# Weights that begin 64 bytes behind a multiple of 2048 bytes in SBUF, beside streamed operands at multiples of it

## The chip, the cores and the metric

The kernel runs on one NeuronCore of one Trainium2 chip. The metric is the time of one execution on the device in microseconds. Before the change it is 2234.84 us, the median of three runs (2234.82 to 2234.86).

## The reference, cut to what matters

A causal convolution of seven taps over the sequence, whose taps are a softmax and are shared by 24 channels each, and behind it a two-layer network with a squared ReLU:

```python
w = softmax(weight)                      # 8 heads x 7 taps
x_pad = concatenate([zeros(B, 6, D), x], axis=1)
y[b, t, h*24 + g] = sum_k w[h, k] * x_pad[b, t + k, h*24 + g]
h = y @ w_in                             # 32768 x 192 times 192 x 2048
r = maximum(h, 0)
out = (s * (r * r) + b) @ w_out          # 32768 x 2048 times 2048 x 192
```

The weights arrive as float64. The result is float32.

## The kernel before, in words

TensorE multiplies in its rounded float32 format (`F32R`), one column of the streamed operand after the other. To keep float32's accuracy every operand is split into a high and a low part, and a product is three matmuls: high by high, high by low, low by high.

Tokens are worked off in 32 blocks of 1024, each as two halves of 512 (`BLK`). The 2048 hidden units are eight groups of 256 (`NPAIR`). A step is one token block `n`, one half `j` and one group `p`. In it

- `first` (line 531) makes the hidden values `h` in PSUM. The operands that stream are the split activations, `sA`, `wA`, `tB` and `wB`; the stationary ones are chunks of 128 columns of `W`. The 192 channels are cut into three pieces of 64 rows, and two pieces are multiplied at the same time, one in rows 0 to 63 of the array, the other in rows 64 to 127. So matmuls come in pairs: 18 matmuls, nine pairs, for each step.
- ScalarE takes ReLU (line 545) and square (line 552), VectorE rounds to the high part `qh` (line 554) and subtracts it to get the low part `ql` (line 559).
- two steps later (`LAG`) `second` (line 614) multiplies `qh` and `ql`, which stream, by the output weights in `W` and `WB`, into accumulators that stay in PSUM over all eight groups: 20 matmuls, ten pairs.

Token block 0 is different: while it runs the weights are converted from the words of float64 to high and low parts (class `Widen`), its second product uses the whole array (`second_whole`, lines 576 to 583), and the convolution of its first blocks is done by TensorE with diagonal matrices (line 257, in plain float32). Later blocks are convolved by VectorE (lines 161 and 163), spread over the steps of the block before. The order of instructions on VectorE, ScalarE and TensorE is that of the program text (`in_order`, `behind`). Each matmul is two instructions on TensorE, a weight load (PEld in the profile) and the streaming of 512 columns (PE); a weight load can run beside the stream of the matmul before it.

Where the tiles lie in SBUF follows from the order of the pools (lines 73 to 89): they are laid end to end in each partition, every tile rounded up to 32 bytes. The tiles of `const` end with one called `gap` that nobody uses; its 296 floats bring the next pool to byte 18432, which is 9 x 2048. All tiles of `qs`, `xs`, `act` and `outs` are 2048 or 4096 bytes long, so each of them, all streamed operands of lines 531 and 614 among them, begins at a multiple of 2048. So does `W`, at byte 139264 (68 x 2048), and `WB` at 180224 (88 x 2048). A row of `W` is 640 floats, 2560 bytes, and a chunk is 512 bytes, so single chunks begin 0, 512, 1024 or 1536 bytes behind a multiple of 2048. `raw`, `wordp` and `xin` follow; the two buffers of `xA` begin at 216064 and 220192 (1024 and 1056 bytes behind a multiple), those of `xB` at 224320 and 226400 (1088 and 1120).

Of the kernel before, what the change touches and what calls it, by code (L numbers as in the profile page):

```python
# [9 lines left out]
F32 = mybir.dt.float32  # L10
# [7 lines left out]
P = 128  # L18
# [9 lines left out]
WARM = (BLK, BLK // 2, BLK // 2)  # L28

GAP = 296  # L30


TOP_MIN = struct.unpack("<f", struct.pack("<I", (1023 - 127) << 20))[0]
# [4 lines left out]
def conv_attention_then_squared_relu_mlp(  # L38
# [41 lines left out]
    bias = const.tile([P, 3], F32, name="bias")  # L80
    const.tile([P, GAP], F32, name="gap")
    qs = ctx.enter_context(tc.tile_pool(name="qs", bufs=LAG + 3))
    xs = ctx.enter_context(tc.tile_pool(name="xs", bufs=2))
    act = ctx.enter_context(tc.tile_pool(name="act", bufs=3))
    outs = ctx.enter_context(tc.tile_pool(name="outs", bufs=3))
    wide_w = ctx.enter_context(tc.tile_pool(name="wide_w", bufs=1))
    raw = ctx.enter_context(tc.tile_pool(name="raw", bufs=2))
    wordp = ctx.enter_context(tc.tile_pool(name="wordp", bufs=3))
# [760 lines left out]
```

## Time and profile before

| | |
|---|---|
| time, median of 3 runs | 2234.84 us |
| the profiled execution's own time | 2234.66 us |
| its span, first to last instruction | 2232.9 us |
| TensorE, streaming | 2226.4 us busy, 19330 matmuls |
| TensorE, weight loads | 1829.1 us busy |
| VectorE | 1753.5 us busy |
| ScalarE | 1286.4 us busy |
| GpSimd | 317.8 us busy |
| mean granted clock of TensorE | 1.000 |
| DMA | 117.5 MB, 53 GB/s on average |

A matmul's duration in the profile runs from the start of its stream to the arrival of its last result, so matmuls that follow each other overlap, and the busy time of TensorE says little about how well it is used; the distance from one start to the next says more. "x" is a count, the figure behind the busy time of a group is the mean of one instruction in ns, and what stands behind the second bar is the idle time ahead of the group and what ended it. In views by line the three figures are the shortest, the median and the longest duration in ns.

### The profile page before, as it was taken

The numbers are of one execution on the slowest core, as the hardware profiler recorded it, in microseconds if no ns is written. First come the engines' busy times: TensorE is split into PE (matmuls) and PEld (weight loads), VectorE is DVE, ScalarE is ACT, GpSimd is POOL, SyncE is SP. The second block draws the span as 40 slices with busy tenths as digits, with TensorE's granted clock in tenths as the row PEclk, the third lists the DMA queues.
The fourth block names the chain that finished last, engine by engine and source line by source line (L and its number), as shares of the span: only waits on it lengthen the run. The fifth ranks groups of instructions, "written<-read, shape, count | busy, mean of one in ns | idle before, by whom it ended". The sixth has DMA issues, their size and how long they took to land.

```text
span 2232.9 us, 45081 instructions
## 1 busy us (share of the span) xinstructions
PE 2226.4 (100%) x19330; PEld 1829.1 (82%) x19330; DVE 1753.5 (79%) x1995; ACT 1286.4 (58%) x1410; POOL 317.8 (14%) x205
## 2 busy tenths in 40 slices
PE   9999999999999999999999999999999999999999
PEld 6788888888888888888888888888888888888887
DVE  8898778777787787777877878778777787787764
ACT  8755555655555555555555555555655555556554
POOL 0022101111011011110110111111101111011110
PEclk9999999999999999999999999999999999999999
DMA  5113112121121111211111111112121121111110
GB/s 180 34 43 87 40 46 62 48 58 44 44 58 53 53 44 45 56 53 53 43 51 50 53 53 53 48 43 62 51 55 44 44 58 53 53 44 42 46 39 17
DMA packets 46168, 117.51 MB, mean 53 GB/s; under 512 B 7760, under 2 KB 8016, under 8 KB 45968
## 3 DMA queue, kind: packets, MB, share of 16 engines
q1 hardware_dynamic: 45824, 114.50, 18.6%
q8 instruction: 151, 2.47, 0.5%
q14 instruction: 49, 0.40, 0.1%
q10 hardware_dynamic: 144, 0.13, 0.0%
HBM read 31.64 MB, written 25.17 MB: 25 GB/s over the span
## 4 chain that ended last, share of the span: by engine, by line
PE 98%; DVE 1%; ACT 1%; DMA 0%; issue 0%; SPq 0%; DVEq 0%
PE acc L614 50%; PE h L531 46%; DVE accA L163 0%; PE acc L576 0%; ACT q L552 0%; DVE ql L559 0%; PE acc L577 0%; PE acc L583 0%; PE acc L582 0%; PE acc L581 0%; ACT qh L554 0%; ACT q L545 0%; DMA xA<-in_xA 0%; DVE t L315 0%; ACT oC L589 0%
## 5 line engine op out<-in xcount | busy, mean ns | idle before, releaser
L545 ACT ACTIVATE q<-h 128x1024 f32<-128x1024 f32 x512 | 525.5, 1026 | 902.8 <-PE h L531 900.4
L559 DVE TENSOR_TENSOR ql<-q,qh 128x1024 fp32r<-128x1024 f32 x512 | 656.7, 1283 | 56.3 <-ACT qh L554 2.6
L554 DVE CAST qh<-q 128x1024 fp32r<-128x1024 f32 x497 | 370.1, 745 | 395.7 <-ACT q L552 393.3
L614 PE MATMUL acc<-qh,W 64*128 64x512 f32 x3960 | 609.9, 386 | 0.0
L552 ACT ACTIVATE q<-q 128x1024 f32<-128x1024 f32 x512 | 543.6, 1062 | 15.9
L614 PEld LDWEIGHTS acc<-qh,W 64*128 64x128 f32 x3960 | 370.9, 184 | 77.9
L531 PE MATMUL h<-sA,W 64*128 64x512 f32 x3072 | 432.4, 387 | 0.0
L531 PE MATMUL h<-wA,W 64*128 64x512 f32 x3072 | 431.6, 386 | 0.0
L531 PE MATMUL h<-tB,W 64*128 64x512 f32 x1536 | 429.9, 386 | 0.0
L531 PE MATMUL h<-wB,W 64*128 64x512 f32 x1536 | 429.9, 386 | 0.0
L614 PE MATMUL acc<-ql,WB 64*128 64x512 f32 x1980 | 385.7, 386 | 0.4 <-DVE ql L559 0.4
L614 PE MATMUL acc<-qh,WB 64*128 64x512 f32 x1980 | 385.6, 386 | 0.0
L614 PE MATMUL acc<-ql,W 64*128 64x512 f32 x1980 | 385.5, 386 | 0.0
L638 POOL TENSOR_TENSOR oB<-oB,oB 128x512 f32<-128x512 f32 x61 | 115.2, 1889 | 1672.7 <-ACT oB L637 1672.7
L163 DVE SCALAR_TENSOR_TENSOR accA<-xA,tap,accA 128x512 f32<-128x512 f32 x378 | 341.5, 903 | 6.8
L531 PEld LDWEIGHTS h<-sA,W 64*128 64x128 f32 x3072 | 287.3, 184 | 62.9 <-issue 1.1
L531 PEld LDWEIGHTS h<-wA,W 64*128 64x128 f32 x3072 | 287.8, 184 | 60.4
L531 PEld LDWEIGHTS h<-tB,W 64*128 64x128 f32 x1536 | 282.6, 184 | 40.5 <-issue 0.2
L531 PEld LDWEIGHTS h<-wB,W 64*128 64x128 f32 x1536 | 282.5, 184 | 20.1
L614 PEld LDWEIGHTS acc<-ql,WB 64*128 64x128 f32 x1980 | 185.5, 184 | 40.1 <-DVE ql L559 1.3
L614 PEld LDWEIGHTS acc<-ql,W 64*128 64x128 f32 x1980 | 185.5, 184 | 39.0
L614 PEld LDWEIGHTS acc<-qh,WB 64*128 64x128 f32 x1980 | 185.5, 184 | 38.8
(115 smaller groups left out, 1035.4 us busy)
## 6 DMA issues: line engine op xcount, KB each, us to landing
wA<-sA SPq DMA_DIRECT2D x126, 256.0 KB, 3.6
outT<-oA SPq DMA_DIRECT2D x63, 256.0 KB, 2.0
wB<-tB SPq DMA_DIRECT2D x60, 256.0 KB, 3.4
xA<-in_xA SPq DMA_DIRECT2D x24, 515.0 KB, 3.6
xB<-in_xB SPq DMA_DIRECT2D x32, 259.0 KB, 2.6
oC<-oB SPq DMA_DIRECT2D x61, 128.0 KB, 2.2
outT<-oC SPq DMA_DIRECT2D x60, 128.0 KB, 2.3
words<-in_w SPq DMA_DIRECT2D x7, 768.0 KB, 6.2
```

What stands on the lines that cost most here:

```text
L163: nc.vector.scalar_tensor_tensor(acc, src, w[:, k : k + 1], acc, op0=ALU.mult, op1=ALU.add)
L531: nc.tensor.matmul(h[:, i, :], w_in(w, p, chunk[0], rows), chunk[part], start=start, stop=stop)
L545: nc.scalar.activation(q, h, AF.Relu)
L552: nc.scalar.activation(q, q, AF.Square)
L554: cast(qh, q)
L559: nc.vector.tensor_tensor(ql, q, qh.bitcast(F32), op=ALU.subtract)
L614: nc.tensor.matmul(accs[to + 2 * i], w(f, r), q[r, f % 2, :], start=start and f == 0, stop=stop and f == ends[i],)
L638: nc.gpsimd.tensor_tensor(o[1], o[1], o[3], op=ALU.add)
```

## The change

A new pool stands between `outs` and `wide_w`. It holds one tile of 16 floats, 64 bytes, in each partition, which no instruction touches.

```diff
 GAP = 296
+SHIFT = 16
...
     outs = ctx.enter_context(tc.tile_pool(name="outs", bufs=3))
+
+    shift = ctx.enter_context(tc.tile_pool(name="shift", bufs=1))
+    shift.tile([P, SHIFT], F32, name="shift")
     wide_w = ctx.enter_context(tc.tile_pool(name="wide_w", bufs=1))
```

All that lies behind it moves up by 64 bytes: `W` begins at 139328 and `WB` at 180288, both 64 bytes behind a multiple of 2048; the scratch of the conversion (`t`, `c`, `words`) and the inputs `xA` and `xB` move too. `qs`, `xs`, `act` and `outs` stay where they were. The instructions of every engine, and their order, are the same as before, row for row. Lines behind the new ones have numbers greater by one (behind line 30) and by four (behind line 85).

## The prediction

> **What bounds the kernel now.** I read the page first, then the waits, the stretches, TensorE's rows in order of time, and the minima and maxima by line.
>
> ```profile
> span 2232.9 us, 45081 instructions
> PE 2226.4 (100%) x19330; PEld 1829.1 (82%) x19330; DVE 1753.5 (79%) x1995; ACT 1286.4 (58%) x1410; POOL 317.8 (14%) x205
> PEclk9999999999999999999999999999999999999999
> PE 98%; DVE 1%; ACT 1%; DMA 0%; issue 0%; SPq 0%; DVEq 0%
> PE acc L614 50%; PE h L531 46%; DVE accA L163 0%; PE acc L576 0%; ACT q L552 0%; DVE ql L559 0%; PE acc L577 0%; PE acc L583 0%; PE acc L582 0%; PE acc L581 0%; ACT qh L554 0%; ACT q L545 0%; DMA xA<-in_xA 0%; DVE t L315 0%; ACT oC L589 0%
> ```
>
> The chain that ends last is TensorE for 98% of the span, at the full granted clock, on two lines: the first products (L531) and the second ones (L614). A busy TensorE isn't proof of a TensorE at its best, so the next question is whether it waits and how evenly it runs.
>
> ```profile
> 100.00:600.00 500.00, 499.92 (x4414) 412.87 (x4414) 407.91 (x467) 282.63 (x305) 81.74 (x50) 1.00 0.20 54
> 600.00:1100.00 500.00, 500.00 (x4414) 413.23 (x4414) 391.77 (x434) 283.94 (x307) 73.31 (x46) 1.00 0.18 50
> 1100.00:1600.00 500.00, 500.00 (x4416) 413.23 (x4414) 395.08 (x441) 281.25 (x303) 71.23 (x45) 1.00 0.19 51
> 1600.00:2100.00 500.00, 500.00 (x4416) 413.23 (x4414) 390.76 (x433) 284.76 (x308) 73.81 (x46) 1.00 0.18 50
> ```
>
> ```profile
> ACT q L545 <- PE h L531: 900.4, 372, 4.5
> DVE qh L554 <- ACT q L552: 393.3, 305, 3.4
> ```
>
> Each of the first four rows is 500 us of the steady part: 4414 matmuls (4416 where two straddle an end), whatever VectorE, ScalarE and the DMA engines do. Matmuls come in pairs, one in each half of the array's rows, that run together. 2 x 500 / 4414 is 226.6 ns a pair. The other two are the waits that bear on it: ScalarE waits 900 us in all for TensorE, VectorE waits behind ScalarE, and TensorE's unbroken busy time shows that it waits for neither. So the time is (number of pairs) x (226.6 ns), plus some 65 us of start and end. Only what changes the 226.6 ns counts.
>
> How much of that time is reading of operands? Each matmul streams 512 columns from SBUF while its successor's 128 columns of weights are loaded. Minima, medians and maxima of both lines, in ns:
>
> ```profile
> L531 PE MATMUL h<-sA,W x3072: 385/386/501, 17.3 to 2219.6; 64*128 64x512 f32 x192
> L531 PE MATMUL h<-wA,W x3072: 385/386/394, 20.0 to 2220.9; 64*128 64x512 f32 x192
> L531 PE MATMUL h<-tB,W x1536: 383/386/498, 19.2 to 2220.3; 64*128 64x512 f32 x192
> L531 PE MATMUL h<-wB,W x1536: 383/386/493, 19.2 to 2220.3; 64*128 64x512 f32 x192
> L614 PE MATMUL acc<-qh,W x3960: 383/386/394, 98.0 to 2225.2; 64*128 64x512 f32 x198
> L614 PE MATMUL acc<-ql,W x1980: 385/386/394, 98.5 to 2225.5; 64*128 64x512 f32 x198
> ```
>
> The duration includes 386 - 226.6 = 159 ns of latency behind the stream, so 386 belongs to the spacing of 226.6. The values above 394 are first ones behind a pause, and their duration contains a weight load. Two things are in these rows. A matmul can take 383 or 394 with the same shape and operands: the spacing isn't a constant of the instruction. And the weights' chunks start at 0, 512, 1024 and 1536 bytes behind a multiple of 2048 (W's rows are 2560 bytes, its chunks 512), yet all medians are 386: steps of 512 bytes make no difference. What 64 bytes do, no row can say.
>
> **What makes the spacing vary.** Behind a pause the matmuls are uneven, then they lock. One full-array piece of block 0, start in us first:
>
> ```profile
> 36.42 0.40 PE L577 MATMUL acc<-ql,WB 128*128 128x512 f32 x1
> 36.66 0.40 PE L576 MATMUL acc<-qh,WB 128*128 128x512 f32 x1
> 36.89 0.40 PE L577 MATMUL acc<-ql,WB 128*128 128x512 f32 x1
> 37.13 0.39 PE L581 MATMUL acc<-qh,W 128*128 128x512 f32 x1
> 37.35 0.39 PE L582 MATMUL acc<-qh,W 128*128 128x512 f32 x1
> ...
> 38.74 0.39 PE L577 MATMUL acc<-ql,WB 128*128 128x512 f32 x1
> ...
> 40.55 0.39 PE L583 MATMUL acc<-ql,W 128*128 128x512 f32 x1
> ```
>
> and as two stretches (length, then TensorE, weight loads, VectorE, ScalarE, GpSimd):
>
> ```profile
> 36.42:38.74 2.32, 2.32 (x12) 1.88 (x10) 2.29 (x5) 2.26 (x3) 0.00 (x0) 1.00 0.00 0
> 38.74:40.55 1.81, 1.81 (x9) 1.50 (x8) 1.81 (x5) 1.81 (x3) 0.00 (x0) 1.00 0.75 231
> ```
>
> In the first stretch ten weight loads stand in 2.32 us: 232.0 ns each, single ones 220 (37.13 to 37.35) to 240. In the second, eight in 1.81 us: 226.3, all alike. The same work on the same addresses costs 5.7 ns more or less by how weight load and stream meet in time. Two more stretches, of pairs:
>
> ```profile
> L531 PE MATMUL h<-wA,W x4: 386/388/392, 24.0 to 24.3; 64*128 64x512 f32 x4
> L531 PEld LDWEIGHTS h<-wA,W x2: 183/184/184, 24.0 to 24.1; 64*128 64x128 f32 x2
> ...
> L531 PE MATMUL h<-wA,W x4: 385/386/386, 26.3 to 26.6; 64*128 64x512 f32 x4
> ```
>
> At 24.0 us one of the two loads came late (24.1 instead of 24.0), and the matmul of its row half took 392 in place of 386: a load at another moment costs its own half of the array 6 ns. The stretch from 26.3 us ends with a pair behind which no load follows until the next wait (the next start is at 26.87), and it took 385: with no load at all, a locked matmul is only 1 ns faster. So most of what lies between 226.6 ns and pure streaming isn't taken by the load in this state.
>
> How far down could it go? The nearest rows with another relation of addresses are the diagonal products of the start (xB begins 1088 bytes behind a multiple of 2048, plus 4 bytes a tap), in plain float32, which take two cycles for each column:
>
> ```profile
> 4.51 6.22 PE L257 MATMUL acc<-xB,q 128*128 128x512 f32 x14
> 10.57 0.59 PE L257 MATMUL acc<-xA,q 128*128 128x512 f32 x1
> ```
>
> ```profile
> L257 PE MATMUL acc<-xA,q x14: 590/592/593, 10.6 to 16.8; 128*128 128x512 f32 x14
> ```
>
> The second view has their durations, nearly alike. 14 of them lie between 4.51 and 10.57 (the first of them includes part of a wait): at most 433 ns each, 216 per 512 cycles. Streaming with these addresses, at half the rate, thus loses little; it is a far row, and a bound.
>
> **The change part by part.** It adds a pool of 64 bytes in each partition that no instruction reads or writes, between the output tiles and W. It adds no instruction, removes none, moves none on any engine, and adds no wait. Three things shift by 64 bytes: the weights W and WB, the scratch of their widening (t, c, words), and the token inputs xA and xB. Streamed operands of the two long lines (sA, wA, tB, wB, qh, ql) lie ahead of the new pool and stay.
>
> Scratch and inputs: nothing. Each converting step of a group of weights (L315 below) comes 7 times at full size, in block 0 alone. The convolution reads xA and xB from two buffers that already differ by 32 bytes modulo 2048, and its groups have one price:
>
> ```profile
> L163 DVE SCALAR_TENSOR_TENSOR accA<-xA,tap,accA 128x512 f32<-128x512 f32 x378 | 341.5, 903 | 6.8
> L315 DVE SCALAR_TENSOR_TENSOR t<-words,t 128x768 int32<-128x768 int32 x7 | 6.7, 959 | 0.2
> ```
>
> ```profile
> xA<-in_xA SPq DMA_DIRECT2D x24, 515.0 KB, 3.6
> ```
>
> They are hidden by TensorE's unbroken work: VectorE is busy 79%, so even 5% on all convolution steps (341.5 us x 0.05 = 17 us over 31 token blocks) stays inside its slack of 480 us. Uncovered, they would cost those 17 us; the loads of xA land in 3.6 us, a whole token block ahead (16 steps of 19 pairs, 16 x 19 x 226.6 ns = 69 us).
>
> Weights: here is the price. Rows that the trace counts on the two lines: 19116 matmuls of 64 rows (3960 + 3 x 1980 on L614, 2 x 3072 + 2 x 1536 on L531), so 9558 pairs; the 168 full-array ones add under 2%, and I leave them out. One nanosecond a pair is 9.6 us. The profiled execution itself took 2234.66 us, 1.8 over its span, against a median of 2234.84: the same within 0.01%, so I subtract from 2234.8.
>
> The trace shows no matmul with this relation of addresses at the full rate, so the change of a pair is bounded from both sides. Below: 226.6 down to 216 (the diagonal row), -10.6 ns, -101 us. Above: up to 232.0 as in the unlocked stretch, +5.4 ns, +52 us. Between them: 0. And the nearest row on the fast side, of this very shape and type with loads running, is the minimum of 383 against 386: -3 ns x 9558 = -29 us. I take that one: the relative phase of load and stream is all that differs between a 383 and a 394, a shift of the weights' addresses changes the bytes that meet at a given phase for every pair, and a locked state settles where the two collide least. That it goes down rather than up is a choice, and the weakest link: the locked state now is already near the low end of 383 to 394.
>
> Forecast: 2234.8 - 29 = **2206 us**.
>
> [...]
>
> **The rivals.**
>
> *Nothing changes.* Mechanism: load and stream don't share what the 226.6 ns are lost on, or what they share repeats every 64 bytes or less. For it: chunks at four offsets of 512 bytes have one median, and the matmul without a load takes 385. Against: the 392 behind a late load. Time: 2234.8, within 4 us.
>
> *The collision goes away altogether.* Mechanism: in the locked state each load hits the stream in the same places, because both begin at multiples of 512, and with 64 bytes between them they never meet. For it: the uneven rows and the 216 of the start, whose streams begin off the multiples. Against: the 385 with no load, and that the diagonal row is at half the rate. Time: 2234.8 - 101 = 2133 us, and VectorE would then be busy 1753.5 / 2133 = 82%, still with room. Between it and the forecast lie states of -5 to -9 ns, 2150 to 2190.
>
> *Slower: the lock is lost.* Mechanism: in the present state the load starts with the stream at equal offsets and stays in step; with 64 bytes between them, the load meets the stream's bytes as the late load did at 24.1 us, on every pair, and the spacing stays at that of the unlocked stretch. It decides as soon as the locked spacing exceeds 226.6. For it: nearly all off-phase matmuls are slower (388 to 394), few faster (383). Price 5.4 ns x 9558 = 52 us: 2287 us; if only half of the pairs are hit, 2261.
>
> *It doesn't do what it says.* The row of 64 bytes could be padded away. The tile sizes leave no room for that: what lies ahead of W adds up to a multiple of 2048, and pools are laid end to end. I give it no chance of its own.
>
> **How the numbers follow.** Forecast (2195 to 2225) 0.33; collision gone or mostly gone (2130 to 2190) 0.20; nothing 0.23; slower 0.24. From 0.2% on, 4.5 us, this kernel's measurement tells a change from none. Faster 0.53, same 0.23, slower 0.24. The forecast's own range is 2195 to 2225; for 8 in 10 it must hold nothing, most of the fast rival and half-hit pairs of the slow one: 2135 to 2270. Left out are the far end of the fast rival and a full loss of the lock.
>
> **What would show it.** Right: in the steady stretches over 4414 matmuls in 500 us (4473 at 223.6 ns a pair), medians of 383 in place of 386 on both lines alike, ScalarE's wait for TensorE down by about 29 us, and the convolution's 903 ns as it was. The last pair ahead of a pause, without a load behind it, tells the part of the stream from that of the load. Wrong: a median of 386 (nothing shared), under 378 (the collision was the whole loss), over 390 (the lock lost), or medians that differ between L531 and L614, which would mean that the offset of the single chunk decides, not the 64 bytes that all have in common.

## The result: 2.8% slower

The changed kernel takes 2297.41 us (median of 4 runs, 2297.34 to 2297.71), the kernel before 2234.83 us on the same chip. The ratio is 1.0281, 95% interval 1.0268 to 1.0294: 62.6 us more. The forecast was 2206 us, the range ended at 2270 us; both missed, and the direction too.

The page of the changed kernel shows the same instructions and a longer TensorE, still at the full granted clock:

```profile
span 2295.9 us, 45081 instructions
PE 2290.0 (100%) x19330; PEld 1838.8 (80%) x19330; DVE 1754.9 (76%) x1995; ACT 1287.8 (56%) x1410; POOL 317.0 (14%) x205
PEclk9999999999999999999999999999999999999999
PE 99%; DVE 1%; DMA 0%; ACT 0%; SPq 0%; issue 0%; DVEq 0%
```

VectorE, ScalarE and GpSimd are as busy as before to within 1.5 us. Two stretches of the steady part (length, TensorE, weight loads, VectorE, ScalarE, GpSimd), and who waits:

```profile
600.00:1100.00 500.00, 500.00 (x4290) 403.57 (x4288) 382.10 (x425) 273.12 (x294) 70.52 (x45) 1.00 0.18 49
1600.00:2100.00 500.00, 500.00 (x4290) 403.57 (x4288) 381.05 (x423) 275.01 (x296) 69.82 (x43) 1.00 0.18 49
```

```profile
ACT q L549 <- PE h L535: 965.4, 375, 4.6
```

4290 matmuls in 500 us instead of 4414: 1000 / 4290 is 233.1 ns a pair, 6.55 more than 226.55. Times 9558 pairs that is 62.6 us, the whole difference. ScalarE waits 965.4 us for TensorE instead of 900.4. The durations (shortest, median, longest in ns):

```profile
L535 PE MATMUL h<-sA,W x3072: 385/392/499, 17.4 to 2282.5; 64*128 64x512 f32 x192
L535 PE MATMUL h<-tB,W x1536: 390/395/492, 19.2 to 2283.2; 64*128 64x512 f32 x192
L618 PE MATMUL acc<-qh,W x3960: 390/392/395, 98.7 to 2288.3; 64*128 64x512 f32 x198
L618 PE MATMUL acc<-ql,WB x1980: 390/395/492, 98.0 to 2287.1; 64*128 64x512 f32 x198
```

Medians are 392 and 395 where 386 stood. A median of 392 is the middle between two durations that take turns. Two neighbouring pairs of the steady part:

```profile
L535 PE MATMUL h<-sA,W x4: 390/392/395, 1000.8 to 1001.0; 64*128 64x512 f32 x4
```

One pair takes 390, the next 395. Of the 17574 matmuls that start between 100 and 2150 us, 8780 take 390 and 8778 take 395, and the pairs start 231 and 236 ns behind each other in turn. So the changed kernel is as regular as the one before, at a higher mean. In order of time, full-array matmuls of block 0 behind the same pause as in the prediction:

```profile
36.70 0.39 PE L581 MATMUL acc<-ql,WB 128*128 128x512 f32 x1
36.93 0.40 PE L580 MATMUL acc<-qh,WB 128*128 128x512 f32 x1
37.16 0.39 PE L581 MATMUL acc<-ql,WB 128*128 128x512 f32 x1
...
38.79 0.40 PE L580 MATMUL acc<-qh,WB 128*128 128x512 f32 x1
...
40.66 0.40 PE L586 MATMUL acc<-qh,W 128*128 128x512 f32 x1
40.90 0.39 PE L587 MATMUL acc<-ql,W 128*128 128x512 f32 x1
```

Durations alternate between 0.39 and 0.40 here too, and the spacing doesn't come down to 226: from 36.70 to 38.79 nine intervals are 232 ns each, from 38.79 to 40.90 nine more are 234. Before, the second half of this piece had come down to 226.3. A pair without a load behind it shows how much of this the load causes; the last pair ahead of that pause, after the change:

```profile
L535 PE MATMUL h<-wA,W x2: 387/387/387, 36.0 to 36.0; 64*128 64x512 f32 x2
```

387, against 385 for such a pair before: most of the loss comes with a running load. What was moved beside the weights kept its price:

```profile
L167 DVE SCALAR_TENSOR_TENSOR accA<-xA,tap,accA 128x512 f32<-128x512 f32 x378 | 340.6, 901 | 6.8
L319 DVE SCALAR_TENSOR_TENSOR t<-words,t 128x768 int32<-128x768 int32 x7 | 6.7, 959 | 0.2
```

### The profile page after: what moved, and what is told of

Read it like the earlier page. It is cut to its first block, busy times and chain, and to the rows that moved or that the text cites. A ratio compares the mean times of both kernels' runs of the same rounds, so it can differ in the third digit from the quotient of the medians.

```text
span 2295.9 us, 45081 instructions
## 1 busy us (share of the span) xinstructions
PE 2290.0 (100%) x19330; PEld 1838.8 (80%) x19330; DVE 1754.9 (76%) x1995; ACT 1287.8 (56%) x1410; POOL 317.0 (14%) x205
## 4 chain that ended last, share of the span: by engine, by line
PE 99%; DVE 1%; DMA 0%; ACT 0%; SPq 0%; issue 0%; DVEq 0%
PE acc L618 50%; PE h L535 47%; PE acc L580 0%; PE acc L586 0%; PE acc L585 0%; PE acc L587 0%; PE acc L581 0%; DVE accA L167 0%; DMA xA<-in_xA 0%; DVE t L319 0%; DVE t L316 0%; DVE t L312 0%; DVE oB L680 0%; ACT W L326 0%; PE acc L677 0%
## 5 line engine op out<-in xcount | busy, mean ns | idle before, releaser
L549 ACT ACTIVATE q<-h 128x1024 f32<-128x1024 f32 x512 | 526.5, 1028 | 965.5 <-PE h L535 965.4
L618 PE MATMUL acc<-qh,W 64*128 64x512 f32 x3960 | 622.9, 392 | 0.0
L535 PE MATMUL h<-sA,W 64*128 64x512 f32 x3072 | 442.2, 393 | 0.0
L535 PE MATMUL h<-wA,W 64*128 64x512 f32 x3072 | 441.6, 392 | 0.0
L535 PE MATMUL h<-tB,W 64*128 64x512 f32 x1536 | 440.0, 393 | 0.0
L535 PE MATMUL h<-wB,W 64*128 64x512 f32 x1536 | 440.0, 393 | 0.0
L618 PE MATMUL acc<-ql,WB 64*128 64x512 f32 x1980 | 392.6, 393 | 0.0
L618 PE MATMUL acc<-ql,W 64*128 64x512 f32 x1980 | 391.9, 392 | 0.0
L618 PE MATMUL acc<-qh,WB 64*128 64x512 f32 x1980 | 391.3, 392 | 0.0
```

The costliest lines, as they stand in the source:

```text
L535: nc.tensor.matmul(h[:, i, :], w_in(w, p, chunk[0], rows), chunk[part], start=start, stop=stop)
L549: nc.scalar.activation(q, h, AF.Relu)
L618: nc.tensor.matmul(accs[to + 2 * i], w(f, r), q[r, f % 2, :], start=start and f == 0, stop=stop and f == ends[i],)
```

## The experiments

The theory formed on this trace is called "distance": weight load and stream read the same partitions, and what counts is the distance between their addresses. Its rivals are the weights' own alignment and the other tiles that moved.

### Which alignment counts

**Everything 64 bytes off.** The edit, on the kernel before:

```diff
-GAP = 296
+GAP = 296 + 16
```

> The unused tile at the end of const is 64 bytes longer and there is no pool ahead of W, so streamed operands, weights, scratch and inputs all begin 64 bytes behind a multiple of 2048. Theory 'distance' (what counts is the distance in bytes between the chunk of weights that is loaded and the operand that streams meanwhile): distance 0 again, pairs of 226.6 ns, 2235 us. Rival 'own alignment' (a chunk of weights that doesn't begin at a multiple of 512 is dearer to load): pairs of 233.1 ns, 2297 us. Rival 'scratch' (what lies behind the weights costs the time): 2297 us.

Measured: 2235.11 us, ratio 1.0001 (0.9990 to 1.0012). The weights lie exactly where the change puts them, and nothing is lost, because the streamed operands moved with them. The weights' own alignment is out, and so is that of the streams.

**Streams off, weights not.** The pool of the weights is made ahead of `qs`, with the unused 64 bytes behind it:

```diff
+    wide_w = ctx.enter_context(tc.tile_pool(name="wide_w", bufs=1))
+    shift = ctx.enter_context(tc.tile_pool(name="shift", bufs=1))
+    shift.tile([P, 16], F32, name="shift")
     qs = ctx.enter_context(tc.tile_pool(name="qs", bufs=LAG + 3))
...
-    wide_w = ctx.enter_context(tc.tile_pool(name="wide_w", bufs=1))
```

> W and WB are placed ahead of the streamed operands, at a multiple of 2048, and 64 unused bytes behind them, so the streamed operands begin 64 bytes behind a multiple and the weights at one: the distance is the negative of the change's. Theory 'distance': not 2235 us; if the sign doesn't matter, 2297 us; if it does, anything from 2150 to 2330 us. Rival 'own alignment' of the weights: 2235 us. Rival 'scratch', which is 64 bytes off here too: 2297 us.

Measured: 2256.07 us, 1.0095 (1.0065 to 1.0124). Slower, but by a third of the change's loss: the distance counts, with its sign.

**Only scratch and inputs off.** The pool `shift` stands behind `wide_w`.

> The 64 unused bytes stand behind W and WB, so only scratch and token inputs shift as in the change; weights and streamed operands lie as before. Theory 'distance' and rival 'own alignment': 2235 us, pairs of 226.6 ns. Rival 'scratch': 2297 us.

Measured: 2234.87 us, 1.0000 (0.9989 to 1.0011). Scratch is out.

**Weights 512 bytes off.** `SHIFT = 128`.

> The unused tile ahead of W has 512 bytes in place of 64. In the trace of before, chunks at all four multiples of 512 behind a multiple of 2048 had a median of 386 ns. Theories 'distance' (which repeats every 512 bytes or less) and 'own alignment': 2235 us. If instead W's begin as a whole has to lie at a multiple of 1024 or 2048: slower by some 60 us, 2297 us.

Measured: 2234.84 us, 1.0000 (0.9988 to 1.0011). Distances that are multiples of 512 are all one, as the medians of the single chunks in the old trace had said.

### How it depends on the distance

The kernel before with a pool of 8, 32, 56, 40, 64 and 112 floats ahead of the weights:

```diff
+    shift = ctx.enter_context(tc.tile_pool(name="shift", bufs=1))
+    shift.tile([P, 8], F32, name="shift")
     wide_w = ctx.enter_context(tc.tile_pool(name="wide_w", bufs=1))
```

> Weights 32 bytes behind a multiple of 2048, streamed operands at multiples. Theory 'distance': some other locked pattern of the pairs; if the loss grows with the distance, between 2235 and 2297 us, about 2266 us (230 ns a pair). If instead only the crossing of a 64-byte boundary counts: 2235 us.

> Weights 128 bytes behind. Theory 'distance': if the loss grows with the distance up to half a period, more than 2297 us; if what collides repeats every 128 bytes, 2235 us, though the change (+64) and the streams at 64 (-64) would then have had one time, which they didn't (2297 and 2256 us).

> Weights 160 bytes behind. Theory 'distance, period of 256 bytes': between the times at 128 (2289 us) and 192 (2256 us), some 2272 us. A time under 2235 us would mean that the present place isn't the best.

> Weights 224 bytes behind a multiple of 2048, that is 32 bytes short of the next multiple of 256. Theory 'distance, period of 256 bytes': on the side of 192 (2256 us) and 256 (2235 us), so between them, some 2245 us, or below both if the best distance isn't 0. If the loss is that of any odd place: 2297 us, as at 32 bytes.

> Weights 256 bytes behind. Theory 'distance' with a period of 256 bytes: 2235 us. With a period of 512: another time, in the span of the unlocked intervals (220 to 236 ns a pair), 2175 to 2325 us.

> Weights 448 bytes behind, which is 64 bytes ahead of the next multiple of 512. Theory 'distance' with a period of 512 or 256 bytes: the time of the streams moved by 64 with the weights at a multiple, 2256 us, and its pairs of 229 ns. If absolute places count besides: another time.

For 16 bytes the weights are views that begin four floats into longer tiles (sixty for `WB`, which gives the same distance modulo 256):

```diff
-    W = wide_w.tile([P, NPAIR, 2, CB], F32R, name="W")
-    WB = wide_w.tile([P, NPAIR, 2, 2 * DB], F32R, name="WB")
+    W = wide_w.tile([P, NPAIR * 2 * CB + 8], F32R, name="W")[:, 4 : 4 + NPAIR * 2 * CB]
+    W = W.rearrange("p (a k c) -> p a k c", a=NPAIR, k=2)
+    WB = wide_w.tile([P, NPAIR * 4 * DB + 64], F32R, name="WB")[:, 60 : 60 + NPAIR * 4 * DB]
+    WB = WB.rearrange("p (a k c) -> p a k c", a=NPAIR, k=2)
```

> W and WB are read 16 bytes behind a multiple of 256, by views that begin four floats into longer tiles. Theory 'distance' with a grain of 16 bytes or less: a loss as at 32 and 224 bytes, 2298 us, or a gain if the best place lies between 0 and 32. With a grain of 32 bytes: 2235 us.

All in one table; the matmuls are those in the stretch from 600 to 1100 us, and the ns of a pair are 1000 us divided by their number.

| weights minus streams, bytes | us | matmuls in 500 us | ns a pair |
|---|---|---|---|
| 0 (before) | 2234.8 | 4414 | 226.6 |
| 16 | 2298.0 | 4288 | 233.2 |
| 32 | 2297.7 | 4290 | 233.1 |
| 64 (the change) | 2297.4 | 4290 | 233.1 |
| 128 | 2288.6 | 4306 | 232.2 |
| 160 | 2297.9 | 4290 | 233.1 |
| 224 | 2297.6 | 4290 | 233.1 |
| 256 | 2234.7 | 4414 | 226.6 |
| 448 | 2255.9 | 4372 | 228.7 |
| 512 | 2234.8 | 4416 | 226.4 |
| -64 (the streams moved) | 2256.1 | 4374 | 228.6 |

Three things follow. The pattern repeats every 256 bytes: 0, 256 and 512 agree (2234.8, 2234.7 and 2234.8 us), and 448 agrees with -64 (2255.9 and 2256.1 us), two layouts that reach the same place modulo 256 in different ways. Distance 0 is the best of all tried; 16 bytes on one side and 32 on the other (16, 224) already cost the full price, so the loss doesn't grow with the distance, and the expectations that interpolated (at 32, 160 and 224 bytes) missed. And 128 isn't a period (2288.6 us).

Dearer places have regular patterns of their own. At -64 three durations take turns; three neighbouring pairs:

```profile
L533 PE MATMUL h<-sA,W x6: 385/388/391, 1000.9 to 1001.3; 64*128 64x512 f32 x6
```

### Where the loss arises

**The load stays in one place.** In the changed kernel, the first product's loads read one column 128 times:

```diff
-        return W[rows, p, part, chunk * P : (chunk + 1) * P]
+        return W[rows, p, part, chunk * P : chunk * P + 1].to_broadcast([HB, P])
```

> The changed kernel, in which the first product's weight loads read one column 128 times over instead of 128 columns (the hidden values are then wrong; the work is the same in number and shape). The load stays at one place in SBUF. Theory 'distance' (the loss arises where the load's walk through SBUF meets the stream's): the pairs of the first product no longer run in the pattern of 230.8 and 235.8 ns that those of the second keep; if the load then collides only once in 256 bytes, they come near the 225 to 227 ns of a stream without a load, 18 matmuls of 38, 2297 - 4600 x 7 ns = 2265 us. If the loss has nothing to do with the addresses that the load reads: 2297 us and one pattern throughout.

Measured: 2289.26 us, 1.0243. Only 8 us of the loss went, where 32 were expected. A load needn't walk to disturb the stream (a median of 390 to 392 for the first product). The same edit on the kernel before, at distance 0:

> The kernel before, in which the first product's weight loads read one column 128 times (the hidden values are then wrong). Distance 0, load at one place. Theory 'in step' (at distance 0 load and stream walk in a fixed relation and hardly meet; a load that stays in one place loses that relation): the first product's pairs go up from 226.7 to about the 231.5 ns of the same load at distance 64, 4600 x 4.8 ns more, 2257 us. Theory 'place' (the start of the load decides alone): 226.7 ns and 2235 us.

Measured: 2254.66 us, 1.0088 (1.0059 to 1.0117). Durations by operand in this kernel:

```profile
L531 PE MATMUL h<-wA,W x3072: 383/392/394, 20.0 to 2240.8; 64*128 64x512 f32 x192
L614 PE MATMUL acc<-qh,W x3960: 383/386/394, 98.2 to 2245.2; 64*128 64x512 f32 x198
```

The first product's median went up to 392 though its loads begin where they did; the second's, whose loads still walk, stayed at 386. 19.8 us over the 4608 pairs of the first product is 4.3 ns each: 230.9 ns, the price that loads in one place have at distance 64 too (8.15 us less than the change's 233.1 over the same pairs is 231.3). So at distance 0 it isn't the place where a load begins that spares the stream, but its walk from there: take that away, by a distance or by a load that stands still, and most of the loss is back (4.3 ns of 6.55). "In step" is only a name for it. By the profile a load takes 184 ns for its 512 bytes, while a stream of 2048 bytes starts every 226.6 ns, so the two don't run side by side at one pace, and no run shows what collides.

**Only the loads of `WB` are off.** 64 unused bytes between `W` and `WB`:

```diff
     W = wide_w.tile([P, NPAIR, 2, CB], F32R, name="W")
+    wide_w.tile([P, 16], F32, name="shift")
     WB = wide_w.tile([P, NPAIR, 2, 2 * DB], F32R, name="WB")
```

> The 64 unused bytes stand between W and WB, so only the 4 loads of WB of the 19 pairs in each step are 64 bytes off. If each pair pays for the load that runs beside it: 4/19 of 62.6 us, 2248 us, and only the streams beside those loads are longer. If one disturbed pair loses the locked pattern for many that follow: up to 2297 us.

Measured: 2260.93 us, 1.0116 (1.0087 to 1.0146), 26 us: twice the share of four pairs in 19. One step of the second product, and the first products behind it:

```profile
L615 PE MATMUL acc<-qh,W x8: 386/390/392, 1001.4 to 1002.3; 64*128 64x512 f32 x8
L615 PE MATMUL acc<-qh,WB x4: 395/395/395, 1000.5 to 1000.9; 64*128 64x512 f32 x4
L615 PE MATMUL acc<-ql,WB x4: 388/389/390, 1000.7 to 1001.2; 64*128 64x512 f32 x4
L615 PE MATMUL acc<-ql,W x4: 390/392/394, 1001.9 to 1002.6; 64*128 64x512 f32 x4
```

```profile
L532 PE MATMUL h<-sA,W x8: 386/386/386, 1002.8 to 1004.8; 64*128 64x512 f32 x8
```

The six pairs with `W`, whose loads are at distance 0, are slow as well (386 to 394), and the next first product's `sA` pairs are all at 386. So disturbed pairs upset those behind them for a while, then the pattern settles again, as behind a pause.

### What the stream loses by itself

A pair without a load had taken nearly as long as one with it (385 for 386 before the change). So the stream itself was changed. In the changed kernel, the first product streams one column 512 times:

```diff
-                    h[:, i, :], w_in(w, p, chunk[0], rows), chunk[part], start=start, stop=stop
+                    h[:, i, :], w_in(w, p, chunk[0], rows),
+                    chunk[part][:, 0:1].to_broadcast([HB, BLK]), start=start, stop=stop
```

> The changed kernel, in which the first product's streams read one column 512 times over (the hidden values are then wrong; the work is the same in number and shape). [...]

Measured: 2220.45 us, 0.9936 (0.9913 to 0.9958). The first product streams at

```profile
L535 PE MATMUL h<-wA,W x3072: 376/376/480, 20.0 to 2206.6; 64*128 64x512 f32 x192
```

10 ns less than the best before, although the loads run on at distance 64. (2297.4 - 2220.5) us over 4608 pairs is 16.7 ns; 233.1 - 16.7 is 216.4. In the kernel before, the stream then ran over 64 columns eight times, and over 4 columns (16 bytes) 128 times:

```diff
-                    h[:, i, :], w_in(w, p, chunk[0], rows), chunk[part], start=start, stop=stop
+                    h[:, i, :].rearrange("p (a c) -> p a c", a=8), w_in(w, p, chunk[0], rows),
+                    chunk[part][:, 0:64].unsqueeze(1).to_broadcast([HB, 8, 64]), start=start, stop=stop
```

> The kernel before, in which the first product's streams read their first 64 columns (256 bytes) eight times over (the hidden values are then wrong). With one column 512 times the pairs took 215.8 ns. If a stream's own loss of 10.8 ns comes with each new line of 16 or 64 bytes: 226.7 ns, 2235 us. If it comes with each new 256 bytes or more: 215.8 ns, 4600 x 10.9 less, 2185 us.

> The kernel before, in which the first product's streams read their first four columns (16 bytes) 128 times over (the hidden values are then wrong). If a stream's own loss comes with each new line of 16 bytes: 215.8 ns a pair, 2185 us. If it comes with each column that differs from the one before: 226.7 ns, 2235 us.

Measured: 2234.77 us (0.9999, 0.9988 to 1.0010) and 2198.81 us (0.9840, 0.9811 to 0.9868). A stream that walks within 256 bytes loses as much as one over 2048 (a median of 386 for both); within 16 bytes it is as fast as on one column (376). The first product by durations in the last of these kernels, and two groups of its second product (busy us, mean ns):

```profile
L531 PE MATMUL h<-wA,W x3072: 375/376/480, 19.5 to 2185.0; 64*128 64x512 f32 x192
```

```profile
L615 PE MATMUL acc<-qh,W 64*128 64x512 f32 x3960 | 613.4, 388 | 0.0
L615 PE MATMUL acc<-ql,WB 64*128 64x512 f32 x1980 | 390.5, 391 | 0.8 <-DVE ql L560 0.8
```

These rows also tell why it wasn't 2185 us: the second product, which the edit leaves alone, went from 386 to means of 388 and 391. That its turns begin out of step is a guess. The last run reads the same 512 columns in another order:

```diff
-                    h[:, i, :], w_in(w, p, chunk[0], rows), chunk[part], start=start, stop=stop
+                    h[:, i, :].rearrange("p (b a) -> p b a", a=2), w_in(w, p, chunk[0], rows),
+                    chunk[part].rearrange("p (a b) -> p b a", a=2), start=start, stop=stop
...
-                    accs[to + 2 * i], w(f, r), q[r, f % 2, :],
+                    accs[to + 2 * i].rearrange("p (a b) -> p a b", a=2), w(f, r),
+                    q[r, f % 2, :].rearrange("p (b a) -> p a b", a=2),
```

> The kernel before, in which the first product streams its two halves of 256 columns interleaved (column 0, 256, 1, 257 and so on), and the second product puts them back by a step of two columns (token block 0 and the last step, which have code of their own, are left in the other order, so their results are wrong). If lines of 16 bytes cost when they are entered: interleaving enters one with every column and a step of two one with every second, so both lines are slower, over 2300 us. If what costs is reading neighbours in a row: below 2235 us.

Measured: 3302.08 us, 1.4777. One half was as expected, the other wasn't:

```profile
L531 PE MATMUL h<-wA,W x3072: 375/376/480, 19.7 to 3284.0; 64*128 64x512 f32 x192
...
L615 PE MATMUL acc<-qh,W x3960: 626/628/636, 98.7 to 3292.3; 64*128 64x512 f32 x198
```

Reading every second column (L615) takes 628 where 386 stood, and the ten pairs of a step 4.50 us in place of 2.27 (1002.37 to 1006.87 us): the spacing nearly doubles. But interleaving two halves that lie 1024 bytes apart (L531), which changes its place in SBUF with every column, takes 376, as little as one column. A kernel in which both products stream like this and the tokens come back in order was not run. From these rows one would estimate 9558 x 10 ns, 96 us under the kernel before; whether the second product and the order of the results allow it is open.

## Why the prediction was wrong

**The bound: right.** The time is the number of pairs times their spacing; 6.55 ns x 9558 is the measured difference. Scratch, inputs, order and other engines cost nothing, as said; the third experiment shows it alone.

**"0, 512, 1024 and 1536 bytes make no difference": right, and nearly the answer.** The period is 256 bytes, so all chunks of the old kernel were at distance 0. The rows therefore compared equal distances with each other, and the trace of before couldn't say what another one costs.

**The failed step is the choice of -3 ns,** "the nearest row on the fast side". The prediction took the fastest single matmul (383) for a state in which all pairs could settle, and named this its weakest link. Read in order of time, the old trace has 383 in six pairs of 9558, each of them the fifth behind a pause. One of them, at 159.2 us, with the pairs ahead of it and behind it:

```profile
L614 PE MATMUL acc<-ql,WB x2: 393/393/393, 158.9 to 158.9; 64*128 64x512 f32 x2
L614 PE MATMUL acc<-qh,W x2: 383/383/383, 159.2 to 159.2; 64*128 64x512 f32 x2
L614 PE MATMUL acc<-qh,W x2: 390/390/390, 159.4 to 159.4; 64*128 64x512 f32 x2
```

The other five stand between 393 and 390 as well. So 383 is a passing value of the uneven stretch behind a pause, whose mean here is 231.9 (158.457 to 160.544 us, nine intervals), and no stretch had settled there. (The 220 in the prediction comes from start times rounded to 0.01 us; single spacings of its stretch, from 36.42 us on, are 224 to 236.) Nor does a pattern settle "where the two collide least": the changed kernel settles at 390 and 395. In place of -3 ns the runs show +6.55 ns; of all distances tried none brought a pair below 226.4.

**The rival that came nearest is the lost lock.** It had the direction and the condition: equal offsets are spared, and 64 bytes between load and stream take that away. The load in one place at distance 0 and the shift of `WB` alone bear this out from two other sides. But the lock isn't lost. Pairs settle into another regular pattern, 390 and 395 in turn, and not into "the unlocked stretch" from which the price of 5.4 ns was taken. It is 6.55, of which 62.6 us follow in place of 52; that the two lie so near is in part luck. The range stopped at 2270 us, which leaves out the full price of this rival. A distance of -64 would have come out inside it (2256 us), and no row that the prediction shows tells the two signs apart. So the rival had the right sign, a price nearly a fifth too low and a chance of 0.24.

**"Most of what lies between 226.6 ns and pure streaming isn't taken by the load": right.** The stream loses about 10 ns by its own walk: 376 for one place, 386 for a walk. The bound of 216 that the diagonal products suggested is real (216.4 with one column; their own 433 ns are 2.00 times that), but the weights' place has no hold on it (376 at distance 64 and at 0).

**"Nothing changes": wrong.** The place of the weights alone is worth 62.6 us, so it bears on the stream. What a stream loses by itself stays open. A unit of 16 bytes, as the expectations suppose it, was the author's assumption: the runs show 376 within 16 bytes and 386 within 256, but also 376 for the interleaved stream, which changes its place with every column, and 628 with a step of two columns. Neither theory on record for that run covers both of its products.

What isn't shown is the mechanism. No run looked inside SBUF, and nothing here says why 192 bytes cost a third of what 64 do (2256.1 and 2297.4 us), nor why interleaving frees the stream.

## What to carry to other kernels

In a kernel like this one, `F32R` matmuls back to back with fresh weights for each, try the same place modulo 256 bytes for weights and streamed operands; an unused tile of 64 bytes in the wrong place cost 2.8%. Other types and shapes were not run. The regular spacing in these traces is a state that the layout sets: of the ten other distances in the table none bettered that of distance 0, and eight settled at a dearer one. A minimum over single instructions isn't a state: look for a stretch that stays there before forecasting it, and for what stands ahead of it and behind it.

## What the runs showed of the hardware

- Distance between weights and streamed operand, modulo 256 bytes: 226.6 ns a pair at 0, 228.7 at 192, 232 to 233 at 16, 32, 64, 128, 160 and 224.
- What the distance sets is a regular pattern of durations: 386 ns throughout at 0; 390 and 395 in turn at 64; 388, 391 and 385 in turn at -64.
- A disturbance outlasts its cause: four shifted loads slowed the six pairs behind them (386 to 394 ns for 386).
- A stream of 512 columns takes 376 ns when it stays within 16 bytes, 386 when it walks, whether over 256 or 2048 bytes, 376 when it alternates between two halves, and 628 with a step of two columns.
